# Second layer: the first product as three row-banded parts on four 32-row bands, expert 0 in 16-bit halves, all engines in program order

## The chip, the cores and the metric

The kernel runs on one core of a Trainium2 chip. Its engines are TensorE (PE, matmuls; PEld is its weight load), VectorE (DVE), ScalarE (ACT), GpSimd (POOL) and SyncE (SP, which issues DMAs). The time is device microseconds of one launch. The median of three runs before the change is 997.73 us (992.65 to 998.36).

## The reference

An mLSTM attention gives x (3072 x 320). A first mixture layer (soft, 8 experts of 4 slots) and a second one follow; the change lies in the second.

```python
def _moe_ref(x, phi, w1, w2):                 # first layer
    logits = x @ phi                          # 3072 x 32
    ...
    slot_out[e] = np.maximum(slot_input[e] @ w1[e], 0.0) @ w2[e]
    ...
    return c @ slot_out                       # c: softmax over the 32 slots

def _moe2_ref(x, w_gate, w1, w2):             # second layer, x = c @ slot_out
    P = np.exp(x @ w_gate - max)
    for _ in range(8):                        # Sinkhorn
        P /= P.sum(1, keepdims=True) + 1e-09
        P /= P.sum(0, keepdims=True) + 1e-09
        P *= N / E
    for e in range(E):                        # 8 experts, w1[e] 320 x 1024, w2[e] 1024 x 320
        h = np.maximum(x @ w1[e], 0.0)
        out += P[:, e:e + 1] * (h @ w2[e])
    return out
```

## The kernel before

The attention and the first layer's logits run up to about 199 us of the span, a tail list (TAIL) up to 207, the first layer's experts up to 237. The rest is the second layer: 48 blocks, n = 0 to 47, of 512 tokens each, six blocks an expert (e, tb = divmod(n, 6)).

The input of the second layer has rank 32: x = c @ slot_out. So x @ w1[e] is computed as c @ S with S = slot_out @ w1[e] (32 x 1024), made by s1_p (col4: four column strips of PE at once, the weights' last 64 rows on 64-row tiles) and s1_c. To keep precision c and S are each split into a rounded half and a rest. cst stacks the rounded c, a copy of it (c_m, on POOL) and the rest of c on 96 partitions; sst stacks the halves of S in the matching order. One 96-row matmul then gives all three parts: z (128 of the 1024 features x 512 tokens). c_p transposes c for a block, c_a and c_d write its halves.

A block runs g1 for eight feature groups kc (one z matmul of 96 rows; ACT writes hh = relu(z) rounded, DVE writes hl, the rest) and g2 for four token tiles tt (24 y matmuls of 320 columns: hh by wh, hh by wl and hl by wh for each kc; then DVE accumulates y into acc with the gate's factor). g1 of block n + 1 is issued in pairs after each g2 of block n. For experts 1 to 7, hh, hl, wh and wl are 16 bit, scaled by powers of two from the absolute maxima of the weights (amax, scales, prep_w2); for expert 0 they are float32r. Gates (gate_p, gate_a, gate_t, gate_d) fill Pm during block 0, and the eight Sinkhorn rounds run in blocks 2 to 5, as sinkhorn_a (row sums, then cl, the column sums, on DVE) and sinkhorn_b (psk, a small PE matmul of cl, then four DVE operations).

What sets the order: PE runs in program order all the time (man). ACT, DVE and POOL run in program order from expert 6 of the first layer to block 1 of the second (man4); after that a scheduler orders them. A PE instruction that waits holds back all that follow.

Of the kernel before, what the change touches and what calls it, by code (L numbers as in the profile page):

```python
# [21 lines left out]
def mlstm_moe_kernel(  # L22
# [37 lines left out]
    CK = 3 * NS  # L60
# [11 lines left out]
    NRB = 5  # L72
# [822 lines left out]
    cst = sm_p.tile([CK, N], F32R, name="cst")  # L895
# [20 lines left out]
    def c_p(gq, pool, tag):  # L916
        pt = pool.tile([P, 512], F32, tag=tag, name="ptc")
        for j in range(TPB):
            nc.tensor.transpose(pt[0:NS, j * P:(j + 1) * P], ct_all[:, gq, j, :], ident)
        tmp["ct", gq] = pt  # L920

    def c_a(gq):
        nc.scalar.copy(out=cst[0:32, gq * TB:(gq + 1) * TB], in_=tmp["ct", gq][0:32, :])

    def c_d(gq):
        cs = slice(gq * TB, (gq + 1) * TB)
        nc.vector.tensor_tensor(
            out=cst[64:96, cs], in0=tmp.pop(("ct", gq))[0:32, :], in1=cst[0:32, cs], op=ALU.subtract,
        )
# [90 lines left out]
    for gq in range(gl):  # L1020
        c_m(gq, gq + 1)
# [72 lines left out]
    wh = {0: wp.tile([P, KF, DM], F32R, name="wh0")}  # L1094
    wl = {0: wp.tile([P, KF, DM], F32R, name="wl0")}

    def prep_w20(k0, k1):
        for kk in range(k0, k1):
            ks = slice(2 * kk, 2 * kk + 2)
            r = w20[0].rearrange("p (k d) -> p k d", d=DM)[:, ks, :]  # L1100
            nc.scalar.copy(out=wh[0][:, ks, :], in_=r)
            nc.vector.tensor_tensor(out=wl[0][:, ks, :], in0=r, in1=wh[0][:, ks, :], op=ALU.subtract)


    scl2 = {}

    def load_w2(e):
        for kk in range(4):
# [5 lines left out]
    def amax(e, kk):  # L1114

        if kk == 0:
            tmp["mx4"] = g_p.tile([P, 2, 4], F32, tag="mx4", name="mx4", bufs=2)
        for a, src in enumerate((m2w[e][:, kk * 640:kk * 640 + 640], raw[:, 2 * kk:2 * kk + 2, :].rearrange("p a d -> p (a d)"))):
            nc.vector.tensor_reduce(  # L1119
                out=tmp["mx4"][:, a, kk:kk + 1], in_=src, axis=AX.X, op=ALU.max, apply_absolute_value=True,  # L1120
            )

    def norm_so():

        nr = g_p.tile([P, 1], F32, name="nr")
        nc.vector.tensor_reduce(out=nr, in_=soa, axis=AX.X, op=ALU.add, apply_absolute_value=True)
        tmp["nso"] = g_p.tile([P, 1], F32, name="nso")
        nc.gpsimd.partition_all_reduce(tmp["nso"], nr, P, bass_isa.ReduceOp.max)

    def scales(e):  # L1130
        mx, mr, iv, sc = (g_p.tile([P, 2], F32, tag=n, name=n, bufs=2) for n in ("mx2", "mr2", "iv2", "sc2"))
        ds = g_p.tile([P, 1], F32, tag="ds2", name="ds2", bufs=2)
        nc.vector.tensor_reduce(out=mx, in_=tmp.pop("mx4"), axis=AX.X, op=ALU.max)  # L1133
        nc.gpsimd.partition_all_reduce(mr, mx, P, bass_isa.ReduceOp.max)  # L1134
        nc.vector.tensor_scalar(
            out=mr[:, 0:1], in0=mr[:, 0:1], scalar1=tmp["nso"], scalar2=4.0, op0=ALU.mult, op1=ALU.mult,
        )
        nc.vector.tensor_scalar(
            out=mr.bitcast(I32), in0=mr.bitcast(I32), scalar1=0x7F800000, scalar2=None, op0=ALU.bitwise_and,
        )  # L1140
        nc.vector.tensor_scalar(
            out=iv, in0=mr, scalar1=1.0 / 16384.0, scalar2=1e-34, op0=ALU.mult, op1=ALU.max,
        )
        nc.vector.reciprocal(sc, iv)
        nc.vector.tensor_tensor(out=ds, in0=iv[:, 0:1], in1=iv[:, 1:2], op=ALU.mult)
        scl2[e] = sc, ds

    def prep_w2(e, k0=0, k1=4):
# [3 lines left out]
        sc = scl2[e][0][:, 1:2]  # L1152
        for kk in range(k0, k1):
            ks = slice(2 * kk, 2 * kk + 2)
            nc.scalar.activation(out=wh[e][:, ks, :], in_=raw[:, ks, :], func=AF.Copy, scale=sc)
            nc.vector.scalar_tensor_tensor(
                out=wl[e][:, ks, :], in0=raw[:, ks, :], scalar=sc, in1=wh[e][:, ks, :],
                op0=ALU.mult, op1=ALU.subtract,
            )

    def scale_p(e):
        nc.vector.tensor_scalar_mul(Ps[:, :, e], Pm[:, :, e], scl2[e][1])

    up(0)
    for e in range(E - 1):
        if e == E - 2:
# [87 lines left out]
    def g1(n, kc):  # L1254
        e, tb = divmod(n, NB)
        if kc == 0:
            hs[n] = tuple(hp.tile([P, KF, TB], F16 if e else F32R, tag=t, name=t) for t in ("hh", "hl"))
        hh, hl = hs[n]
        z = psz.tile([P, TB], F32, tag="z", name="z")
        nc.tensor.matmul(  # L1260
            z, Sst[e][:, kc * P:(kc + 1) * P], cst[:, tb * TB:(tb + 1) * TB], start=True, stop=True,
        )
        nc.scalar.activation(out=hh[:, kc, :], in_=z, func=AF.Relu)  # L1263
        nc.vector.scalar_tensor_tensor(  # L1264
            out=hl[:, kc, :], in0=z, scalar=0.0, in1=hh[:, kc, :], op0=ALU.max, op1=ALU.subtract
        )

    Pm = sm_p.tile([P, NT, E], F32, name="Pm")
    Ps = g_p.tile([P, NT, E], F32, name="Ps")

    y0 = {}

    def g2(n, tt, k0=0, k1=KF):
# [6 lines left out]
        for kc in range(k0, k1):  # L1280
            nc.tensor.matmul(y, hh[:, kc, ts], wh[e][:, kc, :], start=(kc == 0), stop=False)  # L1281
            nc.tensor.matmul(y, hh[:, kc, ts], wl[e][:, kc, :], start=False, stop=False)  # L1282
            nc.tensor.matmul(y, hl[:, kc, ts], wh[e][:, kc, :], start=False, stop=(kc == KF - 1))  # L1283
# [10 lines left out]
        if e == 1:  # L1294
            nc.vector.tensor_scalar_mul(a, a, Pm[:, i, 0:1])
# [6 lines left out]
    def gate_p(gg):  # L1302
# [30 lines left out]
    gm = sm_p.tile([P, 1], F32, name="gm")  # L1333
    ga = sm_p.tile([P, 1], F32, name="ga")
# [129 lines left out]
```

## Time and profile before

| | us |
|---|---|
| median of three runs | 997.73 |
| profiled execution | 996.21 |
| its span, first to last instruction | 994.4 |
| PE busy in the span | 935.0 |
| DVE busy | 656.3 |
| ACT busy | 412.7 |
| POOL busy | 132.5 |

The mean granted TensorE clock is 0.985 of full speed. Matmul records overlap, since matmuls are pipelined, so the distance from one start to the next tells the rate, and the record's length does not.

### The profile page before, as it was taken

To read this page: it belongs to the slowest core of one execution; us is meant where nothing else is said; L and a number is where in the kernel's file an instruction comes from. 1 tells how busy PE (TensorE), PEld (TensorE's weight loads), DVE (VectorE), ACT (ScalarE), POOL (GpSimd) and SP (SyncE) were. 2 spreads that over 40 slices of the span, in tenths; PEclk is the share of its full clock that TensorE was granted. 3 is DMA by queue.
4 is the path that set the end of the run, shared out by engine and by line. 5 is a ranking of instruction groups with operands and counts; after the bars stand their busy time and mean duration, and the time that the engine had idled before them with its cause. 6 is when DMAs were issued, how large, how long until landed. Compare 5 with 4: busy or idle time off the path is not lost.

```text
span 994.4 us, 18368 instructions
## 1 busy us (share of the span) xinstructions
PE 935.0 (94%) x7607; PEld 681.0 (68%) x7607; DVE 656.3 (66%) x1348; ACT 412.7 (41%) x782; POOL 132.5 (13%) x205
## 2 busy tenths in 40 slices
PE   3688888999998999999999999999999999999998
PEld 1477676735987976666666666666666666666665
DVE  6999999835799784666467565756564564545443
ACT  3668777734434222443334342334422442423221
POOL 3677576610000000000000000000000000000000
PEclk9979999999999999999999999999999999999999
DMA  5578887796013000100011010101010000000111
GB/s 93 97 153 158 173 169 181 223 330 210 1 54 106 1 1 1 53 27 28 11 44 53 1 54 1 54 1 54 12 43 1 1 1 2 1 1 28 40 47 47
DMA packets 129605, 63.52 MB, mean 64 GB/s; under 512 B 103507, under 2 KB 123315, under 8 KB 129523
## 3 DMA queue, kind: packets, MB, share of 16 engines
q1 hardware_dynamic: 129523, 62.37, 24.4%
q8 instruction: 59, 0.97, 0.4%
q14 instruction: 23, 0.19, 0.1%
HBM read 58.17 MB, written 4.18 MB: 63 GB/s over the span
## 4 chain that ended last, share of the span: by engine, by line
PE 80%; DVE 15%; issue 3%; ACT 1%; DMA 0%; POOL 0%; SPq 0%; DVEq 0%; POOLq 0%; ACTq 0%
PE y L1281 21%; PE y L1283 21%; PE y L1282 21%; PE z L1260 9%; DVE st L380 3%; DVE W L491 2%; PE pu L1035 2%; DVE st L386 1%; PE pd L1073 1%; DVE amx L346 1%; PE pu L1042 1%; DVE C L519 1%; DVE mx L1119 1%; PE po L544 1%; PE ptk L416 1%
## 5 line engine op out<-in xcount | busy, mean ns | idle before, releaser
L1281 PE MATMUL y<-wx,hh 128*128 128x320 f16 x1344 | 403.9, 301 | 0.0
L1283 PE MATMUL y<-wx,hl 128*128 128x320 f16 x1344 | 401.9, 299 | 0.0
L1282 PE MATMUL y<-wx,hh 128*128 128x320 f16 x1344 | 401.9, 299 | 0.0
L1263 ACT ACTIVATE hh<-z 128x512 f16<-128x512 f32 (+1 forms) x384 | 209.6, 594 | 440.9 <-PE z L1260 440.4
L1264 DVE SCALAR_TENSOR_TENSOR hl<-z,hh 128x512 f16<-128x512 f32 (+1 forms) x384 | 248.2, 686 | 51.1 <-ACT hh L1263 49.1
L1296 DVE SCALAR_TENSOR_TENSOR acc<-y,Ps,acc 128x320 f32<-128x320 f32 x168 | 92.4, 550 | 215.2 <-PE y L1283 214.9
L1281 PEld LDWEIGHTS <-hh 128*128 128x128 f16 x1344 | 131.5, 98 | 89.2 <-issue 43.0
L1283 PEld LDWEIGHTS <-hl 128*128 128x128 f16 x1344 | 131.5, 98 | 51.8 <-DVE hl L1264 1.0
L1282 PEld LDWEIGHTS <-hh 128*128 128x128 f16 x1344 | 132.0, 98 | 44.7
L1260 PE MATMUL z<-cst,sst 96*128 96x512 f32 x384 | 139.5, 442 | 2.4 <-DVE hl L1264 2.3
L1260 PEld LDWEIGHTS z<-cst,sst 96*128 96x128 f32 x384 | 63.3, 191 | 12.7 <-issue 2.9
L1134 POOL PARTITION_ALL_REDUCE mr<-mx x7 | 2.6, 367 | 454.1 <-DVE mx L1133 454.1
L1281 PE MATMUL y<-wh,hh 128*128 128x320 f32 x192 | 61.5, 320 | 0.0
L1283 PE MATMUL y<-wh,hl 128*128 128x320 f32 x192 | 60.8, 317 | 0.2 <-DVE hl L1264 0.2
L1282 PE MATMUL y<-wl,hh 128*128 128x320 f32 x192 | 60.6, 316 | 0.0
L421 ACT COPY T<-ptk 120x1024 f16<-120x1024 f16 x47 | 47.8, 1018 | 17.1 <-PE ptk L416 17.1
L380 DVE SCALAR_TENSOR_TENSOR st<-kq,asc,st 128x320 f16<-128x320 f32 x48 | 40.2, 838 | 2.1 <-ACT st L375 2.1
L416 PE MATMUL ptk<-ident,st 128*120 128x128 f16 x384 | 31.9, 230 | 10.1 <-DVE st L386 6.2
L416 PEld LDWEIGHTS <-st 128*120 128x120 f16 x384 | 30.5, 143 | 14.1 <-issue 5.6
L1282 PEld LDWEIGHTS y<-wl,hh 128*128 128x128 f32 x192 | 37.3, 194 | 0.9
L1281 PEld LDWEIGHTS y<-wh,hh 128*128 128x128 f32 x192 | 37.3, 195 | 0.6
L1283 PEld LDWEIGHTS y<-wh,hl 128*128 128x128 f32 x192 | 37.3, 194 | 0.4 <-DVE hl L1264 0.4
(245 smaller groups left out, 971.9 us busy)
## 6 DMA issues: line engine op xcount, KB each, us to landing
wa<-in_moe_w_dram SPq DMA_DIRECT2D x18, 512.0 KB, 4.5
raw<-in_moe_w_dram SPq DMA_DIRECT2D x28, 320.0 KB
xr<-in_o_gate_dram SPq DMA_DIRECT2D x24, 160.0 KB, 4.7
kq<-in_k_dram SPq DMA_DIRECT2D x24, 160.0 KB, 2.6
kq<-in_q_dram SPq DMA_DIRECT2D x24, 160.0 KB, 3.0
vz<-in_v_dram SPq DMA_DIRECT2D x24, 160.0 KB, 4.1
wb<-in_moe_w_dram SPq DMA_DIRECT2D x6, 640.0 KB, 10.4
out_dram<-acc SPq DMA_DIRECT2D x24, 160.0 KB, 1.8
```

Of the source, the lines that this page charges most:

```text
L380: nc.vector.scalar_tensor_tensor(out=st[:, a, :, lo, :], in0=t[:, a], scalar=sc[:, a:a + 1], in1=st[:, a, :, 0, :], op0=ALU.mult, op1=ALU. ...
L416: nc.tensor.transpose(pt[0:120, h, :], sts[i % (PD - 1)][:, a, h].rearrange("p s d -> p (s d)"), ident16)
L421: nc.scalar.copy(out=t, in_=tmp.pop(("k", a, i))[0:120])
L491: nc.vector.scalar_tensor_tensor(out=Ws[i][:, hh * 4:hh * 4 + 4, :], in0=tmp.pop(("s", i, hh)), scalar=scl[i][:, 0:1], in1=dds.pop((i, hh) ...
L1035: nc.tensor.matmul(dst[32 * j:32 * j + 32, :], lhsT[:, kt, :], v[:, 2 * kt + j // 2, (j % 2) * FQ:(j % 2 + 1) * FQ], start=(kt == 0), stop ...
L1260: nc.tensor.matmul(z, Sst[e][:, kc * P:(kc + 1) * P], cst[:, tb * TB:(tb + 1) * TB], start=True, stop=True,)
L1263: nc.scalar.activation(out=hh[:, kc, :], in_=z, func=AF.Relu)
L1264: nc.vector.scalar_tensor_tensor(out=hl[:, kc, :], in0=z, scalar=0.0, in1=hh[:, kc, :], op0=ALU.max, op1=ALU.subtract)
L1281: nc.tensor.matmul(y, hh[:, kc, ts], wh[e][:, kc, :], start=(kc == 0), stop=False)
L1282: nc.tensor.matmul(y, hh[:, kc, ts], wl[e][:, kc, :], start=False, stop=False)
L1283: nc.tensor.matmul(y, hl[:, kc, ts], wh[e][:, kc, :], start=False, stop=(kc == KF - 1))
L1296: nc.vector.scalar_tensor_tensor(out=a, in0=y, scalar=Ps[:, i, e:e + 1], in1=a, op0=ALU.mult, op1=ALU.add)
```

## The change

The first product no longer stacks its three parts on 96 rows. csh and csr hold the rounded half of c and the rest, each four times, on four bands of 32 partitions; sst holds the halves of S with the feature quarter j on band j. g1 now takes four feature groups at once: 12 matmuls of 32 rows, three for each of four z buffers, in the order part by part, band by band. A block has two such groups, issued after g2 of tiles 0 and 2. psz has four buffers and psy two, instead of three and three. c_p writes each transpose four times, by 16 strip matmuls; c_m goes. The gates take two matmuls a block of tokens, on 64 and on 32 rows.

Expert 0 uses 16-bit halves as the others do, so its maxima, scales and splits come before block 0. The work for the next expert (ahead2) is spread over three blocks, one step after each g2. ACT, DVE and POOL run in program order from expert 3 of the first layer to the end. The ring of weight buffers has four slots instead of five.

```diff
-    NRB = 5
+    NRB = 4
...
         for j in range(TPB):
-            nc.tensor.transpose(pt[0:NS, j * P:(j + 1) * P], ct_all[:, gq, j, :], ident)
+            for g in range(4):
+                nc.tensor.matmul(
+                    pt[NS * g:NS * g + NS, j * P:(j + 1) * P], ct_all[:, gq, j, :], ident,
+                    start=True, stop=True, tile_position=(0, NS * g),
+                )
...
-    psz = ctx.enter_context(tc.tile_pool(name="psz", bufs=3, space=PSUM, reuse_waits="tile"))
-    psy = ctx.enter_context(tc.tile_pool(name="psy", bufs=3, space=PSUM, reuse_waits="tile"))
+    psz = ctx.enter_context(tc.tile_pool(name="psz", bufs=4, space=PSUM, reuse_waits="tile"))
+    psy = ctx.enter_context(tc.tile_pool(name="psy", bufs=2, space=PSUM, reuse_waits="tile"))
...
-    wh = {0: wp.tile([P, KF, DM], F32R, name="wh0")}
-    wl = {0: wp.tile([P, KF, DM], F32R, name="wl0")}
+    wh = {0: wp.tile([P, KF, DM], F16, name="wh0")}
+    wl = {0: wp.tile([P, KF, DM], F16, name="wl0")}
...
-        if e == E - 2:
+        if e == 3:
 
             man4 = tc.manual_schedule(engines={mybir.EngineType.Activation, mybir.EngineType.DVE, mybir.EngineType.Pool})
...
+        for a, kk in {4: ((0, 0), (0, 1), (0, 2)), 5: ((0, 3), (1, 0), (1, 1)), 6: ((1, 2), (1, 3))}.get(e, ()):
+            amax(0, a, kk)
+    amax_all(0, 1)
+    amax_all(0, 0)
...
+    def s1_c(e):
+        (sh, sr), pj, sc = Sst[e], tmp.pop("s1"), sch[e][1]
+        nc.scalar.activation(out=sh, in_=pj, func=AF.Copy, scale=sc)
+        nc.vector.scalar_tensor_tensor(out=sr, in0=pj, scalar=sc, in1=sh, op0=ALU.mult, op1=ALU.subtract)
...
-        z = psz.tile([P, TB], F32, tag="z", name="z")
-        nc.tensor.matmul(
-            z, Sst[e][:, kc * P:(kc + 1) * P], cst[:, tb * TB:(tb + 1) * TB], start=True, stop=True,
-        )
...
+        zs = [psz.tile([P, TB], F32, tag="z", name="z") for _ in range(4)]
+        fs, cs = slice(t * P, (t + 1) * P), slice(tb * TB, (tb + 1) * TB)
+        for a, (w, c) in enumerate(((sh, csh), (sr, csh), (sh, csr))):
+            for j, z in enumerate(zs):
+                r = slice(32 * j, 32 * j + 32)
+                nc.tensor.matmul(
+                    z, w[r, fs], c[r, cs], start=(a == 0), stop=(a == 2), tile_position=(32 * j, 0),
+                )
...
+    KO = [0, 2, 4, 6, 1, 3, 5, 7]
...
+            for a, c in enumerate((csh, csr)):
+                r = NS * (2 - a)
+                nc.tensor.matmul(
+                    tmp["ga", gg], sgs[0:r, (3 - j) * NS:(3 - j) * NS + P],
+                    c[0:r, (b0 + j) * TB:(b0 + j + 1) * TB],
...
+    def ahead2(x):
+
+        for a in range(2):
+            for kk in range(4):
+                yield amax(x, a, kk)
+            amax_all(x, a)
+        yield
+        yield pow2(x, 0)
+        yield pow2(x, 1)
+        s1(x)
+        yield
+        for kk in range(4):
+            yield prep_w2(x, kk)
+        if x + 1 < E:
+            load_m2w(x + 1)
...
         for tt in range(TPB):
             g2(n, tt)
...
-            if n + 1 < NBLK:
-                g1(n + 1, 2 * tt)
-                g1(n + 1, 2 * tt + 1)
...
+            if n + 1 < NBLK and tt % 2 == 0:
+                g1(n + 1, tt // 2)
+            next(steps, None)
 
             st = (n - 1) * TPB + tt
             if 4 <= st < 20:
                 (sinkhorn_b if st % 2 else sinkhorn_a)()
```

How this moves instructions shows at two places. The first is PE in a block of expert 1 or later, between the y matmuls of two token tiles (an instruction of z loads its own weights, and those on 32 rows read csh or csr). Before:

```order
L1282 MATMUL y<-wx,hh 128x320
L1283 LDWEIGHTS hl
L1283 MATMUL y<-wx,hl 128x320
L1260 MATMUL z<-cst,sst 128x512 x2
L1281 LDWEIGHTS hh
L1281 MATMUL y<-wx,hh 128x320
L1282 LDWEIGHTS hh
```

Now:

```order
L1292 LDWEIGHTS hh
L1292 MATMUL y<-wx,hh 128x320
L1293 LDWEIGHTS hl
L1293 MATMUL y<-wx,hl 128x320
L1266 MATMUL z<-csh,sst 128x512 x8
L1266 MATMUL z<-csr,sst 128x512 x4
L1291 LDWEIGHTS hh
L1291 MATMUL y<-wx,hh 128x320
```

Two z matmuls stood there after every g2; now twelve stand there after every other one.

The second place is DVE around the second Sinkhorn sum (rw to cl) of blocks 2 to 5. Before, in the order that the scheduler found:

```order
L1264 SCALAR_TENSOR_TENSOR hl<-z,hh 128x512 x6
L1349 TENSOR_REDUCE rw<-Pm 128x24
L1350 TENSOR_SCALAR rw<-rw 128x24
L1351 RECIPROCAL rw<-rw 128x24
L1352 TENSOR_TENSOR Pm<-Pm,rw 128x192
L1353 TENSOR_REDUCE cl<-Pm 128x8
L1292 COPY acc<-y 128x320
L1264 SCALAR_TENSOR_TENSOR hl<-z,hh 128x512 x2
```

Now, in program order:

```order
L1302 COPY acc<-y 128x320
L1272 SCALAR_TENSOR_TENSOR hl<-z,hh 128x512 x4
L1103 TENSOR_REDUCE mx_4265<-raw 128x1
L1362 TENSOR_REDUCE rw<-Pm 128x24
L1363 TENSOR_SCALAR rw<-rw 128x24
L1364 RECIPROCAL rw<-rw 128x24
L1365 TENSOR_TENSOR Pm<-Pm,rw 128x192
L1366 TENSOR_REDUCE cl<-Pm 128x8
L1302 COPY acc<-y 128x320
L1103 TENSOR_REDUCE mx_4265<-raw 128x1
L1371 TENSOR_SCALAR ca<-psk 128x8
```

The sum stands behind four hl of a group and a maximum (mx) that belongs to expert 1, and the two accumulations of a group's tiles stand on both sides of it. On PE, psk follows the y matmuls of the tile after the group, with no z between them.

## Rows read from the trace of the kernel before

**Rows 1.** Busy time by engine in stretches, with instruction counts, granted clock and DMA share.

```profile
core 0: us, PE busy (x) PEld busy (x) DVE busy (x) ACT busy (x) POOL busy (x), PEclk, DMA share, GB/s
...
207.00:240.00 33.00, 31.06 (x383) 12.44 (x382) 12.22 (x28) 10.56 (x26) 1.22 (x3) 0.95 0.86 273
...
260.50:354.00 93.50, 87.86 (x565) 83.31 (x565) 79.48 (x185) 32.42 (x60) 1.49 (x4) 0.96 0.14 43
354.00:990.00 636.00, 636.00 (x4497) 437.14 (x4496) 364.93 (x632) 215.22 (x397) 1.43 (x4) 1.00 0.07 23
```

**Rows 2.** Timeline of PE in a steady stretch: start, length, line, operation, operands.

```profile
503.08 0.30 PE L1282 MATMUL y<-wx,hh 128*128 128x320 f16 x1
...
506.07 0.30 PE L1283 MATMUL y<-wx,hl 128*128 128x320 f16 x1
506.09 0.73 PE L1260 MATMUL z<-cst,sst 96*128 96x512 f32 x2
506.67 0.31 PE L1281 MATMUL y<-wx,hh 128*128 128x320 f16 x1
```

**Rows 3.** Timeline of the weight loads (PEld) in the same stretch.

```profile
506.07 0.33 PEld L1260 LDWEIGHTS z<-cst,sst 96*128 96x128 f32 x2
```

**Rows 4.** Timeline of PE around the strips that make S for expert 2.

```profile
401.51 0.30 PE L1283 MATMUL y<-wx,hl 128*128 128x320 f16 x1
401.74 1.07 PE L1035 MATMUL pu<-wa,soT 128*32 128x256 f32 x16
402.74 0.64 PE L1042 MATMUL pu<-wa,soT 64*32 64x256 f32 x8
403.31 0.73 PE L1260 MATMUL z<-cst,sst 96*128 96x512 f32 x2
403.88 0.31 PE L1281 MATMUL y<-wx,hh 128*128 128x320 f16 x1
```

**Rows 5.** The 64-row tail of the strips: shortest, median, longest, first and last start.

```profile
L1042 PE MATMUL pu<-wa,soT x8: 376/388/400, 402.7 to 403.0; 64*32 64x256 f32 x8
```

**Rows 6.** Waits of PE from 260 to 354 us: total, times, longest.

```profile
engine line waited for: us in total, times, longest us
PE psk L1357 <- DVE cl L1353: 3.2, 2, 1.7
```

**Rows 7.** Timeline of all engines in block 1, DVE and ACT after a pair of z.

```profile
262.82 0.34 DVE L1349 TENSOR_REDUCE rw<-Pm 128x24 f32<-128x192 f32 x1
...
264.07 0.63 PE L1260 MATMUL z<-cst,sst 96*128 96x512 f32 x2
264.13 0.55 DVE L1353 TENSOR_REDUCE cl<-Pm 128x8 f32<-128x192 f32 x1
...
264.56 1.09 ACT L1263 ACTIVATE hh<-z 128x512 fp32r<-128x512 f32 x2 [2.26 <-PE z L1260]
...
265.19 1.29 DVE L1264 SCALAR_TENSOR_TENSOR hl<-z,hh 128x512 fp32r<-128x512 f32 x2
...
266.40 0.81 DVE L1119 TENSOR_REDUCE mx<-wa 128x1 f32<-128x640 f32 x1
```

**Rows 8.** Busy time and clock in the 5 us after a wait of psk.

```profile
310.00:315.00 5.00, 5.00 (x25) 4.91 (x24) 3.83 (x10) 0.21 (x1) 0.00 (x0) 0.66 0.00 0
```

**Rows 9.** Timeline of PE at that wait.

```profile
308.98 0.39 PE L1357 MATMUL psk<-cl,ones 128*128 128x8 f32 x2 [1.65 <-DVE cl L1353]
309.22 0.40 PE L1281 MATMUL y<-wh,hh 128*128 128x320 f32 x1
```

**Rows 10.** Timeline of PE: the first y of block 1 and of block 6.

```profile
260.56 0.31 PE L1281 MATMUL y<-wh,hh 128*128 128x320 f32 x1
...
353.51 0.30 PE L1281 MATMUL y<-wx,hh 128*128 128x320 f16 x1
```

**Rows 11.** Timeline: the last two sums of the first layer on DVE, the first z.

```profile
233.10 0.55 DVE L1084 SCALAR_TENSOR_TENSOR soa<-pd,emask,soa 128x320 f32<-128x320 f32 x1 [2.60 <-PE pd L1073]
...
235.27 0.55 DVE L1084 SCALAR_TENSOR_TENSOR soa<-pd,emask,soa 128x320 f32<-128x320 f32 x1 [0.64 <-PE pd L1073]
...
240.24 0.70 PE L1260 MATMUL z<-cst,sst 96*128 96x512 f32 x2
```

**Rows 12.** Timeline of PE: two transposes of c in the tail.

```profile
198.38 1.05 PE L919 MATMUL ptc<-ident,ct_all 128*32 128x128 f32 x8
```

More of the change, by code (lines that the diff above doesn't have):

```diff
@@ L1112, in load_w2, with prep_a @@
             )
[L1114 to L1148, printed above, removed]
+    KP = [slice(0, 3, 2), slice(4, 7, 2), slice(1, 4, 2), slice(5, 8, 2)]
+    def prep_a(e, kk):
         if e not in wh:
@@ L1151, in prep_w2, with prep_d @@
             wh[e], wl[e] = wx[:, a, :, :], wx[:, a + 1, :, :]
[L1152 to L1159, printed above, removed]
+        nc.scalar.activation(out=wh[e][:, KP[kk], :], in_=src2[e][:, KP[kk], :], func=AF.Copy, scale=scw[e][1])
+    def prep_d(e, kk):
+        nc.vector.scalar_tensor_tensor(
+            out=wl[e][:, KP[kk], :], in0=src2[e][:, KP[kk], :], scalar=scw[e][1], in1=wh[e][:, KP[kk], :],
+            op0=ALU.mult, op1=ALU.subtract,
+        )
+    def prep_w2(e, kk):
+        prep_a(e, kk)
+        prep_d(e, kk)
     def scale_p(e):
-        nc.vector.tensor_scalar_mul(Ps[:, :, e], Pm[:, :, e], scl2[e][1])
+        nc.vector.tensor_scalar(
+            out=Ps[:, :, e], in0=Pm[:, :, e], scalar1=sch[e][0], scalar2=scw[e][0], op0=ALU.mult, op1=ALU.mult,
+        )
     up(0)
     for e in range(E - 1):
-        if e == E - 2:
+        if e == 3:
             man4 = tc.manual_schedule(engines={mybir.EngineType.Activation, mybir.EngineType.DVE, mybir.EngineType.Pool})
@@ L1183, in mlstm_moe_kernel @@
     c_p(gl, psp, "p")
+    pow2(0, 1)
+    prep_a(0, 0)
     down_d(E - 1)
+    norm_so()
     soT = sm_p.tile([P, 3, NS], F32, name="soT")
@@ L1279, in g2 @@
         y = y0[tt]
-        for kc in range(k0, k1):
-            nc.tensor.matmul(y, hh[:, kc, ts], wh[e][:, kc, :], start=(kc == 0), stop=False)
+        for k in range(k0, k1):
+            kc = KO[k]
+            nc.tensor.matmul(y, hh[:, kc, ts], wh[e][:, kc, :], start=(k == 0), stop=False)
             nc.tensor.matmul(y, hh[:, kc, ts], wl[e][:, kc, :], start=False, stop=False)
-            nc.tensor.matmul(y, hl[:, kc, ts], wh[e][:, kc, :], start=False, stop=(kc == KF - 1))
+            nc.tensor.matmul(y, hl[:, kc, ts], wh[e][:, kc, :], start=False, stop=(k == KF - 1))
         if k1 < KF:
@@ L1380, in mlstm_moe_kernel @@
+    for k in range(KF):
+        if k == 3:
+            g1(0, 1)
+        for tt in range(2):
+            g2(0, tt, k, k + 1)
+        if k == 3:
+            gate_p(0)
             gate_a(0)
-        elif kc == 1:
+        elif k == 5:
             gate_t(0)
             gate_d(0)
-        elif kc == 3:
-            gate_p(1)
-            gate_a(1)
-        elif kc == 4:
-            gate_t(1)
-            gate_d(1)
-        elif kc == 5:
-            gate_m()
-        if kc >= G1K:
-            g1(1, kc - G1K)
@@ L1394, in mlstm_moe_kernel @@
-    g2(0, TPB - 1)
-    for kc in range(KF - G1K, KF):
-        g1(1, kc)
+    gate_p(1)
+    gate_a(1)
+    g2(0, 2)
+    gate_t(1)
+    gate_d(1)
+    g1(1, 0)
+    g2(0, 3)
+    gate_m()
+    g1(1, 1)
     gate_e()
     NBLK = E * NB
+    def ahead2(x):
[12 more added lines that the diff above has]
+            load_m2w(x + 1)
@@ L1399, in mlstm_moe_kernel @@
     for n in range(1, NBLK):
         e, tb = divmod(n, NB)
-        if tb == 1 and 0 < e < E - 1:
-            load_w2(e + 1)
-            for kk in range(4):
-                amax(e + 1, kk)
-            scales(e + 1)
-            prep_w2(e + 1)
-        if tb == 4 and 0 < e < E - 1:
-            scale_p(e + 1)
+        if tb == (1 if e == 0 else 0) and e + 1 < E:
+            if e > 0:
+                load_w2(e + 1)
+            steps = ahead2(e + 1)
+        if tb == 0 and e > 0:
+            if e == 1:
+                scale_p(0)
+            scale_p(e)
@@ L1430, in mlstm_moe_kernel @@
                 (sinkhorn_b if st % 2 else sinkhorn_a)()
-                if st == 19:
-                    scale_p(1)
-        if n == 1:
-            man4.__exit__(None, None, None)
+    for x in steps:
+        pass
+    man4.__exit__(None, None, None)
     man.__exit__(None, None, None)
```

164 lines of the change are left out of this document (71 added, 93 removed).

## Prediction

> **What bounds the kernel now.** I read the stages first, then one steady stretch, then the waits of expert 0. By stage [rows 1], TensorE (PE) is busy 636.0 of 636.0 us between 354 and 990 us, at a granted clock of 1.00: experts 1 to 7 of the second layer, 42 blocks of 512 tokens. Nothing on VectorE (DVE) or ScalarE (ACT) counts there unless it grows by half; only what PE issues does. Between 260.5 and 354 us, blocks 1 to 5 of expert 0, PE is busy 87.86 of 93.50 us, so 5.6 us are waits.
>
> The steady stretch gives the price list [rows 2]. Second-product matmuls start every 0.136 us (503.08 to 506.07 holds 22 of them). The last before a pair of first-product matmuls starts at 506.07 and has streamed by 506.21; the next y starts at 506.67. So a pair costs 0.46 us between the streams, 0.48 counted by the 3.74 us period less 24 x 0.136. A block has 96 y matmuls and four pairs: 13.04 + 1.92 = 14.96 us. The pair's weight load is free, because it starts at 506.07 [rows 3], together with the last y.
>
> **The main term: the first product.** Before, 8 matmuls of 512 columns a block, 4 pairs. After, two groups of 12 on four 32-row bands. If the four bands run together, that is 3 rounds a group, 6 a block instead of 8. The trace has no bands of 32 rows with 128 columns. The nearest rows are the column strips of the first product's input and its 64-row tail [rows 4, 5]: 16 matmul records in four rounds take 1.00 us until the next shape starts, 8 in two rounds take 0.57. Two equations give a round of 0.215 us and 0.14 us for each change of shape. The 0.14 is a drain (y starts at 401.51, has streamed by 401.65, the strips start at 401.74: 0.09), the first weights (32 columns) and the issue. So four tiles do run at once, in the tail even on two different row bands [rows 5]: eight records start within 0.3 us.
>
> What a band group costs, by these: entry drain 0.09; first weights, now 128 columns, 0.11 (the pair after the strips takes 0.57 from 403.31 to 403.88 [rows 4], against 0.46 where its load was hidden); 0.02 issue; three rounds 0.645; exit drain 0.09; 0.03 for the first y weights. Sum 0.99 us, against 0.96 for the two pairs that it replaces. The two rounds saved in a block (0.43 us) are spent on four shape changes, each with a drain and with a weight load in the open. 84 groups belong to experts 1 to 7: 84 x 0.03 = **+2.4 us**. Bounds: with no drain and no issue a group is 0.107 + 0.645 + 0.03 = 0.78; one matmul after another it is 12 x 0.215 + 0.32 = 2.9. I take 0.99, since the strip rows are the same engine changing shape.
>
> A rule stands against one step of this. The pair's weights loaded under a y matmul on the same rows [rows 3], so I let rounds two and three hide their loads. The Trainium skill, "TensorE: Matmul & The Clock Gate", section "Part 3: Packing small matmuls", says that a load overlaps matmuls in flight only where its row group differs. By it each round would pay its load, 0.107 + 0.215, and a group 1.20 us; the rows speak against it here.
>
> **The order of work in blocks 1 to 5.** This is the second term, and the order rows show it. Each of eight Sinkhorn rounds has a column sum on DVE (cl), which PE's small psk matmul waits for, in PE's program order. Before, a scheduler set DVE's order and put most sums early; two waits of psk remained, 3.2 us together [rows 6]; the rest of the 5.6 us is a wait for z's buffers. After, DVE's order is the program's: accumulate, four hl, a maximum or a weight split, then the five Sinkhorn operations. From the end of a band group: ACT starts 0.27 us later (z at 264.07, streamed by 264.29, ACT at 264.56), hl starts 0.63 after ACT, four hl take 4 x 0.645 = 2.58 (a pair 1.29), a maximum 0.81, the sum from rw to the end of cl 1.86 (262.82 to 264.68) [rows 7]. That is 6.15 us. PE has only 24 x 0.136 = 3.26 us of work before psk, so it waits 2.9. By block: block 2 (maxima) 2 x 2.9; block 3: 2.1 (no step), then 1.1 (four small operations for a scale, some 0.7, an estimate from the four that take 1.31 between 262.82 and 264.13; but 1.8 us of strips lie ahead of psk); block 4 (weight splits, taken like a maximum) 2 x 2.9; block 5 2 x 2.1. Sum 19 us where 5.6 were.
>
> After psk's wait of 1.65 us [rows 9] the granted clock was 0.66 over the 5 us from 310 [rows 8], a mean of its two levels, 2.4 and 1.2 GHz: 1.7 us lost. The wait for z's buffers was followed by a like stretch, psk's other wait by none. Of the new waits seven are of 2 us or more; I take 9 us, between 0 and 14 (8 x 1.7).
>
> Expert 0's second product goes from float32r, 0.146 us a matmul (260.56 to 264.07 holds 24 [rows 7, 10]), to 16 bit at 0.136. Blocks 1 to 5 after: 5 x (13.04 + 2 x 0.99) = 75.1, the strips for expert 1 1.8 (403.88 - 401.51 less the usual 0.60), waits 19, psk itself 8 x 0.24 = 1.9 (308.98 to 309.22 [rows 9]), clock 9: 106.8. Before: 353.51 - 260.56 = 93.0 [rows 10]. **+13.8 us.** Who is late next after a wait: nobody, since DVE and ACT then stand idle until the next group.
>
> **Join and block 0.** Expert 0 now needs powers of two before its first split. Eight maxima sit between the down sums on DVE, from expert 4 on. Two of them, two clears and four small operations stand between expert 6's sum, which ended at 233.65, and the last one, which started at 235.27 [rows 11]: 2 x 0.81 + 0.34 + 0.7 puts it at 236.3, and soT and the first z (240.24) follow 1.0 us later. Then the z group needs both halves of the split (0.4 + 0.5, an estimate from hh and hl, which take 0.545 and 0.645 for twice the columns), and the pipeline starts with ACT's start, hh and hl in a row (0.27 + 0.63 + 0.65). The gates are 12 matmuls on 64 and 32 rows instead of 6 on 96: 12 x 0.215 without and 12 x 0.41 with a shape change each; I take 3.7. The second half of the split is then there at 241.2, and two rounds and a drain later, at 241.8, the first z: 1.6 + 13.04 + three groups 2.97 + gates 3.7 + their transposes 0.8 = 263.9 for block 1, against 260.56: **+3.5 us** (2 to 6). One weight buffer fewer (NRB 4) I cost at nothing: the queues have 14% free between 207 and 240 us [rows 1]; if that cover fails, 4.6 us (14% of 33) is the most that a fuller queue can take.
>
> **The tail of the first layer.** Each of six transposes becomes 16 strip matmuls. Two old ones took 1.05 us [rows 12], 0.53 each; a new one 4 x 0.215 + 0.14 = 1.0. Six times 0.5 is 3; half to all of it is in front of something that waits. **+2.0 us** (0 to 3). The copies by GpSimd vanish, off the path: nothing.
>
> **Sum.** 2.0 + 3.5 + 13.8 + 2.4 = 21.7 on the profiled execution's 996.2 us: **1018 us**. The median of the runs is 997.7, 1.5 above the profiled one. What a measurement here can tell from no change is about 1%.
>
> **Rivals.**
> - Not slower: PE doesn't drain between y and the bands and issues without a gap, so a group costs 0.78. Then 96 x 0.21 = 20 us come back: 998. It decides from 0.77 downward. For it: the 96-row pair enters and leaves without a drain [rows 2]. Against it: the gaps of 0.09 around every strip group [rows 4]. Chance 0.12.
> - Loads show in every round, group 1.20: 96 x 0.21 = +20, 1038. For it: no row has two loads of 128 columns in two bands. Against it: [rows 3]. Chance 0.08; this is the time that the rule above gives. A figure of the same section, 3.07 times for four bands of 512 columns, would give a group of about 1.2 as well.
> - Loads of the four bands go one after another: 12 x 0.107 + 0.215 + 0.21 = 1.71, +69 us: 1087. Strip loads, each of 32 columns, don't queue so [rows 5]. Chance 0.10.
> - The change doesn't do what it says, and the bands run in turn: 2.9 a group, +183 us: about 1200. Chance 0.04.
> - The Sinkhorn sums come early enough: -28 us (19 + 9), 990. For it: only two of eight psk waits showed before [rows 6]. Against it: its order, by which 0.9 + 2.58 + 1.86 us of work stand against PE's 3.26. Chance 0.06.
>
> **How the numbers follow.** The forecast has 0.60, and its own range is 1005 to 1026 (clock 0 to 14, tail and join by their bounds). With the first two rivals that is 0.80: 997 to 1040. Faster by over 1% (below 986): half of the last rival and corners of the first, 0.06. Within 1%: the rest of these and the low corner of the forecast, 0.17. Slower: 0.77.
>
> **What would show it.** Steady block 15.0 us with z in two bursts of about 0.65 us; starts of four z matmuls a few ns apart; a gap of 0.09 us on both sides. psk in blocks 2 to 5 waiting for cl eight times, 17 to 21 us in all, and a granted clock below 1.00 after some. First y of block 1 near 266 us. Wrong if a steady block is under 14.7 or over 15.5 us, or if psk waits under 8 us in all.

## The result and the profile after

The change makes the kernel slower: 1011.1 us in the median of four runs (1005.8 to 1011.7) against 996.7 before, ratio 1.014 with an interval of 1.010 to 1.018. In a second comparison the same kernel (again, below) took 1009.9 against 995.9, ratio 1.0153 (1.0129 to 1.0177). So the change costs some 14 us. 1018 was forecast, with a range of 997 to 1040. The profiled execution after took 1005.8 us, its span 1004.1; it was the shortest of its runs.

Where the time went, stage by stage, from timelines of the two kernels (the first column after is this profile; "again" is the second profiled execution of the changed kernel). The bounds of a stage are the start of the last-but-one sum of the attention (sacc), of the copies siT and soT on DVE (the transposed inputs and outputs of the first layer's slots), and of the first y of blocks 1, 6 and 47.

| stage, us | before | after | again | forecast of the change |
|---|---|---|---|---|
| start to sacc | 198.5 | 194.5 | 196.8 | none |
| sacc to siT (tail) | 8.7 | 10.1 | 10.1 | +2.0 |
| siT to soT (experts, join) | 29.6 | 29.7 | 29.8 | +1.0 |
| soT to block 1 (block 0) | 23.8 | 29.1 | 29.2 | +2.5 |
| blocks 1 to 5 | 93.0 | 96.8 | 96.6 | +13.8 |
| blocks 6 to 46 | 624.2 | 627.2 | 627.2 | +2.4 (to the end) |

The first row is not the change's: in the eleven profiles of the changed kernel and its edits (below), which share this stage, sacc starts anywhere from 194.5 to 199.8 us, and the 198.5 before lies among them. An operation on DVE that runs 48 times in it (st from kq) took 838 ns each before, 784 and 781 ns in the two profiles after. Without that row the change costs 13.7 us by either profile (9.7 + 4.0 and 12.0 + 1.7, from spans of 994.4, 1004.1 and 1006.4), about what the medians say.

The four rows of the timeline of DVE and PE that bound the early stages after (answering [rows 10, 11]):

```profile
194.50 0.55 DVE L699 SCALAR_TENSOR_TENSOR sacc<-sacc,sc,pq 128x321 f32<-128x321 f32 x1
...
204.58 0.26 DVE L995 TENSOR_TENSOR siT<-ptf,rs 128x96 f32<-128x96 f32 x1
...
234.29 0.26 DVE L1201 COPY soT<-pt_so 128x96 f32<-128x96 f32 x1 [0.45 <-PE pt_so L949]
...
263.40 0.31 PE L1291 MATMUL y<-wh,hh 128*128 128x320 f16 x1
```

**The steady group.** The timeline of PE after, where [rows 2] stood before, and of the weight loads, where [rows 3] stood:

```profile
524.71 0.30 PE L1293 MATMUL y<-wx,hl 128*128 128x320 f16 x1
524.94 0.74 PE L1266 MATMUL z<-csh,sst 32*128 32x512 f32 x8
525.51 0.40 PE L1266 MATMUL z<-csr,sst 32*128 32x512 f32 x4
525.84 0.31 PE L1291 MATMUL y<-wx,hh 128*128 128x320 f16 x1
```

```profile
524.58 0.10 PEld L1293 LDWEIGHTS <-hl 128*128 128x128 f16 x1
524.94 0.30 PEld L1266 LDWEIGHTS z<-csh,sst 32*128 32x128 f32 x8 [0.26 <-issue]
525.28 0.20 PEld L1266 LDWEIGHTS z<-csr,sst 32*128 32x128 f32 x4
```

From the end of a y (524.71 + 0.136) to the next y at 525.84 a group takes 0.99 us, the forecast's number. Its parts: 0.09 until the first loads, twelve matmuls in three rounds, and at the end a y whose own load starts in the open. The loads of the second round, in a narrower window, start at 525.05, while the first round streams on the same rows:

```profile
525.05 0.19 PEld L1266 LDWEIGHTS z<-csh,sst 32*128 32x128 f32 x4
```

So rounds two and three hide their loads. By the rule that was weighed in the prediction (the Trainium skill, "TensorE: Matmul & The Clock Gate", section "Part 3: Packing small matmuls") they would not, and this trace contradicts it. A steady block takes 15.05 us, 14.96 before.

**The waits.** The waits of PE after from 200 to 380 us (answering [rows 6]), and DVE and PE at one of the eight:

```profile
PE psk L1370 <- DVE cl L1366: 15.0, 8, 2.5
```

```profile
283.58 2.48 DVE L1272 SCALAR_TENSOR_TENSOR hl<-z,hh 128x512 f16<-128x512 f32 x4 [1.03 <-ACT hh L1271]
285.98 0.81 DVE L1103 TENSOR_REDUCE mx<-raw 128x1 f32<-128x640 f32 x1
286.71 0.34 DVE L1362 TENSOR_REDUCE rw<-Pm 128x24 f32<-128x192 f32 x1
...
288.03 0.49 DVE L1366 TENSOR_REDUCE cl<-Pm 128x8 f32<-128x192 f32 x1
```

```profile
286.00 0.30 PE L1293 MATMUL y<-wh,hl 128*128 128x320 f16 x1
288.67 0.36 PE L1370 MATMUL psk<-cl,ones 128*128 128x8 f32 x2 [2.37 <-DVE cl L1366]
288.88 0.30 PE L1291 MATMUL y<-wh,hh 128*128 128x320 f16 x1
```

DVE does not pause between 283.58 and the sum: it is late by its order, four hl and a maximum ahead of the sum, and PE has run out of y at 286.00. What followed the waits is in a table by stretch (columns as in [rows 1]; the 5 us behind three of the eight waits, then blocks 1 to 5, then the steady part):

```profile
288.70:293.70 5.00, 5.00 (x43) 3.34 (x44) 2.25 (x7) 0.47 (x1) 0.00 (x0) 1.00 0.00 0
299.00:304.00 5.00, 5.00 (x43) 3.33 (x44) 2.23 (x7) 0.49 (x1) 0.38 (x1) 1.00 0.02 5
...
329.00:334.00 5.00, 5.00 (x26) 3.17 (x26) 1.83 (x6) 0.00 (x0) 0.00 (x0) 0.66 0.00 0
...
263.40:360.19 96.79, 81.82 (x645) 53.55 (x641) 65.28 (x154) 26.38 (x50) 0.76 (x2) 0.98 0.09 28
...
365.00:980.00 615.00, 615.00 (x4967) 413.84 (x4965) 358.58 (x645) 186.78 (x354) 4.53 (x12) 1.00 0.08 25
```

Of the eight stretches behind a wait one shows the low clock of [rows 8], 0.66, the other seven 1.00. That is 1.7 us (0.34 x 5), where the forecast took 9.

### The profile page after: what moved, and what is told of

The parts are those of the page before. It is cut to its first block, busy times and chain, and to the rows that moved or that the text cites. A ratio compares the mean times of both kernels' runs of the same rounds, so it can differ in the third digit from the quotient of the medians.

```text
span 1004.1 us, 20232 instructions
## 1 busy us (share of the span) xinstructions
PE 936.5 (93%) x8549; PEld 642.4 (64%) x8549; DVE 646.0 (64%) x1363; ACT 378.8 (38%) x728; POOL 132.4 (13%) x205
## 4 chain that ended last, share of the span: by engine, by line
PE 76%; DVE 12%; ACT 2%; issue 2%; DMA 1%; SPq 0%; POOL 0%; DVEq 0%; ACTq 0%
PE y L1291 21%; PE y L1293 20%; PE y L1292 20%; PE z L1266 9%; DVE hl L1272 2%; DVE W L490 2%; DVE st L379 2%; DMA big<-in_moe_w_dram 1%; PE pu L1034 1%; DVE st L385 1%; DVE C L518 1%; DVE amx L345 1%; PE po L543 1%; ACT hh L1271 1%; PE po L551 1%
## 5 line engine op out<-in xcount | busy, mean ns | idle before, releaser
L1271 ACT ACTIVATE hh<-z 128x512 f16<-128x512 f32 x384 | 198.3, 602 | 490.6 <-PE z L1266 490.6
L1272 DVE SCALAR_TENSOR_TENSOR hl<-z,hh 128x512 f16<-128x512 f32 x384 | 238.5, 683 | 93.2 <-ACT hh L1271 93.1
L1291 PEld LDWEIGHTS <-hh 128*128 128x128 f16 x1536 | 151.1, 98 | 93.4 <-issue 37.4
L1292 PEld LDWEIGHTS <-hh 128*128 128x128 f16 x1536 | 150.7, 98 | 54.6
L1266 PE MATMUL z<-csh,sst 32*128 32x512 f32 x768 | 71.0, 441 | 0.6 <-ACT sst L1217 0.6
L1291 PE MATMUL y<-wh,hh 128*128 128x320 f16 x192 | 58.9, 307 | 0.7 <-ACT hh L1271 0.7
L1293 PE MATMUL y<-wh,hl 128*128 128x320 f16 x192 | 58.8, 306 | 0.3 <-DVE hl L1272 0.3
L1292 PE MATMUL y<-wl,hh 128*128 128x320 f16 x192 | 58.8, 306 | 0.0
L420 ACT COPY T<-ptk 120x1024 f16<-120x1024 f16 x47 | 47.8, 1017 | 14.9 <-PE ptk L415 14.8
L1266 PEld LDWEIGHTS z<-csh,sst 32*128 32x128 f32 x768 | 29.1, 183 | 26.2 <-issue 24.3
L1266 PE MATMUL z<-csr,sst 32*128 32x512 f32 x384 | 38.7, 392 | 0.0
L415 PEld LDWEIGHTS <-st 128*120 128x120 f16 x384 | 29.7, 140 | 13.4 <-issue 5.5
L543 PE MATMUL po<-vz,W 128*64 128x41 f32 x768 | 32.2, 234 | 5.6 <-DVE y L569 2.6
L490 DVE SCALAR_TENSOR_TENSOR W<-pss,aiv,dd 128x512 f32<-128x512 f32 x48 | 35.5, 740 | 1.1 <-PE pss L484 1.0
```

What stands on the lines that cost most here:

```text
L415: nc.tensor.transpose(pt[0:120, h, :], sts[i % (PD - 1)][:, a, h].rearrange("p s d -> p (s d)"), ident16)
L420: nc.scalar.copy(out=t, in_=tmp.pop(("k", a, i))[0:120])
L490: nc.vector.scalar_tensor_tensor(out=Ws[i][:, hh * 4:hh * 4 + 4, :], in0=tmp.pop(("s", i, hh)), scalar=scl[i][:, 0:1], in1=dds.pop((i, hh) ...
L543: nc.tensor.matmul(po[TH * a:TH * a + TH, gg, j * D1:(j + 1) * D1], Ws[i][:, h, TH * a:TH * a + TH], own_v(vz[i % NV], h, 1).rearrange("p ...
L1266: nc.tensor.matmul(z, w[r, fs], c[r, cs], start=(a == 0), stop=(a == 2), tile_position=(32 * j, 0),)
L1272: nc.vector.scalar_tensor_tensor(out=hl[:, kc, :], in0=z, scalar=0.0, in1=hh[:, kc, :], op0=ALU.max, op1=ALU.subtract)
```

## The experiments

All are edits of the changed kernel. Times are medians, ratios are to the kernel before on the same chip, with 95% intervals.

| run | us | ratio |
|---|---|---|
| again | 1009.9 | 1.0153 (1.0129 to 1.0177) |
| sums_early | 990.1 | 0.9953 (0.9936 to 0.9971) |
| two_parts | 987.6 | 0.9932 (0.9910 to 0.9954) |
| extra_shape | 1034.2 | 1.0398 (1.0378 to 1.0418) |
| extra_same | 1014.0 | 1.0191 (1.0168 to 1.0214) |
| band_major | 1011.5 | 1.0171 (1.0150 to 1.0192) |
| rows96 | 987.9 | 0.9931 (0.9913 to 0.9949) |
| gates128 | 987.7 | 0.9932 (0.9910 to 0.9955) |
| rows96_late | 991.9 | 0.9972 (0.9957 to 0.9987) |
| rows96_join | 984.4 | 0.9902 (0.9881 to 0.9923) |

### again: the changed kernel once more

No edit. 

> The changed kernel once more, for a second profile and interval. In the profiled execution (1005.8 us) the clock cost only some 3 us in blocks 1 to 5 and the attention stage was 4 us shorter than before; the other executions of it took about 1011 us at a lower mean clock. If the psk waits cost clock, this profile shows a time near 1011 with more stretches below full clock behind psk in blocks 2 to 5, the stage 5 to 10 us longer. If the difference is the attention stage's own spread, blocks 1 to 5 take the same 96.8 us and the attention stage is longer.

Blocks 1 to 5 took 96.6 us with 14.9 us of waits in eight, as in the first profile. The attention was 2.3 us longer than there: the difference between the two profiles lies in the attention, not in the clock behind psk. One stretch of eight shows the low clock here too, but another one: it follows the first wait (PE's starts 2.66 us apart), and the longest (2.80) is followed by 1.00. The waits, and the 5 us behind these two:

```profile
PE psk L1370 <- DVE cl L1366: 14.9, 8, 2.5
```

```profile
291.20:296.20 5.00, 5.00 (x26) 3.15 (x26) 1.72 (x6) 0.00 (x0) 0.00 (x0) 0.69 0.00 0
333.00:338.00 5.00, 5.00 (x42) 3.35 (x43) 2.33 (x7) 0.46 (x1) 0.00 (x0) 1.00 0.00 0
```

### sums_early: DVE's sums ahead of hl

```diff
             g2(n, tt)
+            st = (n - 1) * TPB + tt
+            if 4 <= st < 20 and st % 2 == 0:
+                sinkhorn_a()
             if n + 1 < NBLK and tt % 2 == 0:
                 g1(n + 1, tt // 2)
...
-            st = (n - 1) * TPB + tt
-            if 4 <= st < 20:
-                (sinkhorn_b if st % 2 else sinkhorn_a)()
+            if 4 <= st < 20 and st % 2:
+                sinkhorn_b()
```

> The changed kernel with the five DVE operations of each Sinkhorn sum ahead of the next group's hl in program order, and nothing else moved. If the order of DVE makes psk wait (theory), the eight waits of 15 us in all go to under 3 us, with them the slow stretches behind them, and the kernel gains 13 to 20 us on the changed one: 991 to 998 us, the same as before the change within 1%. Rival: DVE is full in blocks 2 to 5, and the wait moves to hl or to z's buffers; then it gains less than 6 us.

20 us back, with the same instructions. DVE after the edit, and blocks 1 to 5 in the table by stretch:

```profile
289.53 0.34 DVE L1362 TENSOR_REDUCE rw<-Pm 128x24 f32<-128x192 f32 x1
...
290.85 0.50 DVE L1366 TENSOR_REDUCE cl<-Pm 128x8 f32<-128x192 f32 x1
291.26 2.47 DVE L1272 SCALAR_TENSOR_TENSOR hl<-z,hh 128x512 f16<-128x512 f32 x4
```

```profile
270.45:348.75 78.30, 78.30 (x644) 53.02 (x641) 63.86 (x153) 26.39 (x50) 0.76 (x2) 1.00 0.11 35
```

The sum stands ahead of hl, PE is busy 78.30 of 78.30 us, and no psk waits. So the order of DVE made the waits, and waits and clock together were 96.8 - 78.3 = 18.5 us. hl can stand back here: its z is needed a block later.

### two_parts: one round fewer in every group

```diff
-        for a, (w, c) in enumerate(((sh, csh), (sr, csh), (sh, csr))):
+        for a, (w, c) in enumerate(((sh, csh), (sr, csh))):
```

(with stop at a == 1.) 

> The changed kernel without the third part of the first product (rounded half of S by the rest of c): 8 band matmuls a group instead of 12, so the result lacks that part. Theory: a group is 0.35 us of shape changes, first weights and issue, and 0.22 us a round; one round less saves 96 x 0.22 = 21 us, to about 990. If the cost went by matmul (issue or loads in turn), 4 of 12 of about 1.0 us would go, 32 us. If drains and loads alone made it, under 10 us.

The steady block fell from 15.05 to 14.59 us, 0.23 for each of its two groups. A group now takes 0.76 us from the end of a y (520.24 + 0.136) to the next, where it took 0.99:

```profile
520.24 0.30 PE L1293 MATMUL y<-wx,hl 128*128 128x320 f16 x1
520.47 0.74 PE L1266 MATMUL z<-csh,sst 32*128 32x512 f32 x8
521.14 0.31 PE L1291 MATMUL y<-wx,hh 128*128 128x320 f16 x1
```

Four matmuls of 512 columns a round on four bands thus take what one took in [rows 2] (0.24, half a pair): the bands run at once, and "in turn", "loads in turn" (0.43 a round for the loads alone) and "loads in every round" (0.32) fall.

### extra_shape and extra_same: the price of a change of shape

Both put a matmul of 32 columns between two y streams, behind tiles 1 and 3, 94 in all; one is on 32 rows, the other on 128.

```diff
+            elif n + 1 < NBLK:
+                xp = psp.tile([P, TB], F32, tag="p", name="xp")
+                nc.tensor.matmul(
+                    xp[:, 0:32], Sst[e][0][0:32, 0:P], csh[0:32, 0:32], start=True, stop=True, tile_position=(0, 0),
+                )
```

> The changed kernel with one more matmul of 32 rows and 32 columns behind the y matmuls of tiles 1 and 3 in every block but the last (94 in all), where no group stands; its output is not used. Theory: two shape changes, one load of 128 columns in the open and a few ns of matmul: 0.09 + 0.11 + 0.02 + 0.09 + 0.03, about 0.33 us each, +31 us, to about 1042. If the change of shape drains nothing, 0.05 to 0.14 us each: +5 to +13 us.

> The changed kernel with one more matmul at the same 94 places as extra_shape, 32 columns wide too, but on all 128 rows, so that no shape changes; its output is not used. There an extra matmul cost 0.30 us between the y streams. Theory: the shape changes and the load in the open make that price; without them the load hides under the last y matmul and an extra costs 0.03 to 0.08 us, +3 to +8 us on the changed kernel (1010). Rival: any float32r matmul between 16-bit ones costs about the same, +20 us or more.

On 32 rows it cost 24 us, on 128 rows 4, by the medians against those of again. The intervals of extra_same and again overlap; the steady block tells them apart, 15.13 us against 15.05. PE in the first, its load, and PE in the second:

```profile
546.16 0.30 PE L1293 MATMUL y<-wx,hl 128*128 128x320 f16 x1
546.39 0.28 PE L1435 MATMUL xp<-csh,sst 32*128 32x32 f32 x1
546.60 0.31 PE L1291 MATMUL y<-wx,hh 128*128 128x320 f16 x1
```

```profile
546.38 0.18 PEld L1435 LDWEIGHTS xp<-csh,sst 32*128 32x128 f32 x1 [0.26 <-issue]
```

```profile
543.87 0.30 PE L1293 MATMUL y<-wx,hl 128*128 128x320 f16 x1
543.90 0.29 PE L1435 MATMUL xp<-csh,sst 128*128 128x32 f32 x1
544.04 0.31 PE L1291 MATMUL y<-wx,hh 128*128 128x320 f16 x1
```

On 128 rows the load starts at 543.87, with the last y and under it, and the gap is 0.03 us. On 32 rows it is 0.30 us between the y streams: 0.09 until the load starts, the load in the open (0.11 by [rows 4]), and about 0.1 more until the next y, which would be the drain on the way back. The length of a steady block says about the same: 15.68 us with two, 15.05 without. The whole kernel lost 24 us and not the 31 expected, since blocks 1 to 5 took no longer (95.7 us): there psk waited 13.2 us instead of 15.0, and no wait was followed by the low clock. That closes the account of the first product: six rounds of 0.23 are 1.38 us a block, two visits of 0.30 make it 1.98, and the block has 15.05 - 13.04 = 2.01. Before it was 1.92. What two rounds fewer give, 0.54, the two visits take (0.6).

### band_major: the twelve matmuls band by band

```diff
-        for a, (w, c) in enumerate(((sh, csh), (sr, csh), (sh, csr))):
-            for j, z in enumerate(zs):
+        for j, z in enumerate(zs):
+            for a, (w, c) in enumerate(((sh, csh), (sr, csh), (sh, csr))):
```

> The changed kernel with the two loops over parts and bands exchanged: all three parts of a band before the next band, the same 12 matmuls. Theory: matmuls start in program order, and the second part of a band waits for its first, so the bands no longer overlap in full; a group goes from 1.0 toward 2.9 us, at the most +180 us; with the third part of a band beside the first of the next, ten rounds, about 2.5 us and +145 us. Rival: order does not matter, since the engine finds what can run; no change.

I expected the bands to run in turn; that was wrong. Almost nothing changed (a steady block 15.09 us against 15.05). In the program csh, csh and csr of band 0 stand ahead of the first csh of band 1; in the timeline all csh start ahead of any csr:

```profile
522.04 0.30 PE L1293 MATMUL y<-wx,hl 128*128 128x320 f16 x1
522.26 0.76 PE L1266 MATMUL z<-csh,sst 32*128 32x512 f32 x8
522.83 0.42 PE L1266 MATMUL z<-csr,sst 32*128 32x512 f32 x4
523.19 0.31 PE L1291 MATMUL y<-wx,hh 128*128 128x320 f16 x1
```

The exchanged order did reach the engine: the first matmuls of the four bands start 10 ns apart here (522.265 to 522.295) and 3 ns apart in the changed kernel (524.941 to 524.951), as fits two more matmuls between them.

### rows96: the 96-row z in the new order

The first product, the gates and the buffers as before, but program order, expert 0 in 16 bit, and the early sums.

```diff
-    csh = sm_p.tile([P, N], F32R, name="csh")
-    csr = sm_p.tile([P, N], F32R, name="csr")
+    cst = sm_p.tile([3 * NS, N], F32R, name="cst")
...
+        z = psz.tile([P, TB], F32, tag="z", name="z")
+        nc.tensor.matmul(
+            z, Sst[e][:, kc * P:(kc + 1) * P], cst[:, tb * TB:(tb + 1) * TB], start=True, stop=True,
+        )
```

> Program order for all engines, 16-bit halves for expert 0 and the early Sinkhorn sums, but the first product on 96 rows as before the change (three copies of c instead of four, a pair of z after every g2, three z and three y buffers, gates as before). Theory: a steady block is 14.96 us instead of 15.05 (-4 us), block 0 loses the shape changes of gates and groups (-4 to -6 us): 980 to 986 us, about 1.3% faster than before the change. Rival: the narrow writes of S (twelve small operations an expert in program order) hold DVE and ACT, and blocks 2, 8, 14 and so on lose 1 us or more each.

A steady block is 14.96 us again, blocks 6 to 46 take 623.3 us against 627.2: the bands lose 3.9 us there. The total missed the expectation (980 to 986) by some 2 us. In block 0 PE stood idle (below), and the granted clock was 0.50 from 246 to 252 us; how much is due to each was not separated:

```profile
243.04 0.70 PE L1267 MATMUL z<-cst,sst 96*128 96x512 f32 x2 [1.18 <-DVE sst L1221]
244.06 0.47 PE L1267 MATMUL z<-cst,sst 96*128 96x512 f32 x1 [0.31 <-DVE sst L1221]
246.54 0.45 PE L1290 MATMUL y<-wh,hh 128*128 128x320 f16 x1 [2.01 <-ACT hh L1270]
248.33 0.45 PE L1292 MATMUL y<-wh,hl 128*128 128x320 f16 x1 [1.08 <-DVE hl L1271]
```

### rows96_late: the same with the sums late

The edit of sums_early undone in rows96. 

> rows96 with the Sinkhorn sums back behind hl and the step, as in the change. Theory: the wait of psk comes from the work that program order puts ahead of the sum. With a pair of z after every tile only two hl stand there: 0.27 + 0.63 + 1.29 + 0.8 + 1.86 = 4.9 us against 3.26 + 0.46 us of PE work, a wait of 1.1 us where a step stands and 0.4 where none does; eight waits of 6 to 8 us in all, and rows96_late is 5 to 9 us slower than rows96 (988). Rival: the band groups make the waits; then there is no difference.

It costs 4 us (the two intervals don't overlap; blocks 1 to 5 take 82.0 us for 78.3), where the same order cost 20 us with the bands: psk waits 3.2 us in four waits instead of 15.0 in eight. That is less than the 5 to 9 us, and half of the waiting, that were expected.

```profile
PE psk L1366 <- DVE cl L1362: 3.2, 4, 1.5
```

With pairs only two hl (1.29 us) stand ahead of the sum, with groups four (2.48). Most of the loss in blocks 1 to 5 so belongs to the late sums and the groups of four together.

### gates128: the gate matmuls on 128 rows, with the early sums

```diff
-                    tmp["ga", gg], sgs[0:r, (3 - j) * NS:(3 - j) * NS + P],
-                    c[0:r, (b0 + j) * TB:(b0 + j + 1) * TB],
-                    start=(j == 0 and a == 0), stop=(j == n - 1 and a == 1), tile_position=(0, 0),
+                    tmp["ga", gg], sg_[:, (3 - j) * NS:(3 - j) * NS + P], c[:, (b0 + j) * TB:(b0 + j + 1) * TB],
+                    start=(j == 0 and a == 0), stop=(j == n - 1 and a == 1),
```

> sums_early with the gates' 12 matmuls on 128 rows, the weights of the unused rows zero, so that no gate matmul changes the shape. They stood 0.43 us apart on 64 and 32 rows in turn. Theory: 0.215 to 0.24 each, block 0 gets 2 to 3 us shorter; the whole kernel 987 us against 990, within what the intervals can tell. Rival: the gates wait for something else there, and block 0 keeps its length.

PE's timeline, first of the changed kernel, then of this one:

```profile
243.97 0.49 PE L1319 MATMUL pgl<-csh,sgs 64*128 64x512 f32 x1
244.40 0.49 PE L1319 MATMUL pgl<-csr,sgs 32*128 32x512 f32 x1
244.81 0.49 PE L1319 MATMUL pgl<-csh,sgs 64*128 64x512 f32 x1
```

```profile
246.12 0.40 PE L1321 MATMUL pgl<-csr,sgr 128*128 128x512 f32 x1
246.36 0.39 PE L1321 MATMUL pgl<-csh,sgs 128*128 128x512 f32 x1
```

0.42 us apart where the rows change between 64 and 32, 0.24 where they stay: 12 matmuls save some 2.2 us. The total's gain over sums_early is as large (2.5 us by the medians, 2.1 by the ratios, as the chips differ), but the intervals of the two overlap.

### rows96_join: rows96 with the start of block 0 interleaved by hand

```diff
-    for kc in range(3):
-        g1(0, kc)
-    prep_w2(0, 2)
-    prep_w2(0, 3)
+    s1_c(0, (1,), False)
+    g1(0, 0)
+    g1(0, 1)
+    prep_w2(0, 1)
+    s1_c(0, (2,), False)
+    g1(0, 2)
```

(False: the copy of the third part goes to GpSimd; the other two splits and preparations follow inside the loop over kc.) 

> rows96 with the start of block 0 interleaved by hand: a quarter of S, two z, the next quarter, and the weight splits behind them, the third copies on GpSimd. In rows96 PE stood still for some 6 us between the strips of S and the first y matmuls. Theory: 3 to 5 us of that go, 983 to 985 us. Rival: the splits of expert 0's weights are what block 0 waits for, and they only move: within 1 us of rows96.

984.4 us, 1% under the kernel before, the lowest median of all, and within what was expected. Its first y stands 1.58 us behind the first z, 3.50 in rows96. By the ratios the gain over rows96 is 2.9 us, and the intervals of the two overlap a little.

## Why the forecast was right, step by step

**The main term** was right in size and in mechanism: 0.99 us a group by the trace, four bands at once, loads hidden in rounds two and three, a drain and a load in the open on each visit. One step of it was given no reason: the round of 0.215 us was read from strips of 256 columns and used for bands of 512. It held (0.23 by two_parts), as half a pair, 0.24, would have suggested; but the prediction does not argue it so, and that part is luck. All four rivals about the group fall: no drain (0.09 is there, extra_shape), loads in every round and loads in turn (525.05, two_parts), bands in turn. Blocks 6 to 46 lost 3.0 us against before and 3.9 against rows96, for a forecast of 2.4.

**Blocks 1 to 5** were right in mechanism (DVE's program order, shown by sums_early) and wrong in size: +3.8 us for +13.8. The step that went wrong in size is "I take 9 us, between 0 and 14" for the clock: in either profile one wait of eight was followed by the low clock, 1.7 us. The rate came from three waits of the kernel before, two of them followed by the low clock, which is too few. The length of a wait does not decide: in the first profile the low clock followed the longest (PE's starts 2.80 us apart) and none of three of 2.65 to 2.68 us, in the second one of 2.66 and not the one of 2.80. What decides stays open. The waits were also smaller, 15.0 us by the trace where 17 to 21 was to be the sign: the starts around them stand 1.00 to 2.80 us apart, 17.4 us for eight, less 0.136 each 16.3 us for a forecast of 19, in part since four hl take 2.48 and a maximum gives way after 0.73, not 2.58 and 0.81, and since PE starts its 24 y some 0.12 us behind the end of the last band matmul (the way back, which the group's price has and this sum left out). The rest of the sum held: 75.1 + 1.8 + 1.9 = 78.8 forecast without waits and clock, 78.3 in sums_early.

**Join and block 0** were +5.4 for +3.5 (the sum there, 263.9 - 260.56, is 3.3). The join was nothing (0.1 for 1.0): the last sum of the first layer came 3.3 us after the one before it, 2.2 before the change, as the maxima between them would have it; but that one came 1.0 us sooner behind siT. Why it did was not tried. Block 0 was +5.3: the gates took the upper of the two bounds (0.42 us each, 12 x 0.41, where I took 3.7 us in all), and the clock granted was 0.72 from 246 to 252 us, which had no term:

```profile
246.00:252.00 6.00, 6.00 (x27) 3.53 (x27) 0.56 (x2) 0.59 (x1) 0.00 (x0) 0.72 0.00 0
```

The y there start 0.27 us apart from 247.46 on, just behind the gates, at 1.2 GHz. That the gates cause it is only a guess. For it: gates128 shows 1.00 from 240 to 258 us. Against it: sums_early had 0.50 from 240 to 246 us, ahead of them, and rows96, with the gates on 96 rows as before, 0.50 from 246 to 252, ahead of its gates too. The cause stays open, and these are single profiles.

**The tail** was +1.4 for +2.0.

The rival "sums early enough" did not happen, and sums_early shows that it was priced right (990 forecast, 990.1). In all the forecast's 21.7 us were 8 too many: 10.0 in blocks 1 to 5 (7.3 for the clock, 2.7 for the waits) and 1.5 in the tail and the join, against 2.8 too few in block 0 and 0.6 in the steady part. That these partly cancel is luck. The weight buffers (four instead of five) and the z and y buffers were not tried by themselves; the stage of the first layer's experts, which reads the ring, took as long as before (29.7 us for 29.6).

## What to carry to other kernels

Row tiling pays by the rounds that it saves, less what it costs to change the shape and back: here 0.23 us a round against 0.30 us a visit, so two rounds saved in two visits give nothing. By these prices products of one shape should stand together, so that fewer visits are paid; that was not tried. Where engines run in program order, a small result that another engine waits for belongs ahead of bulk work that is needed a block later; five small instructions moved past four large ones were worth 20 us here, about what the tiling could have saved with free changes of shape (two rounds of 0.23 us in each of 48 blocks, 22 us).

## What was not expected of the hardware

The engine does not hold a matmul for a free band behind one for a busy band: in band_major all four bands started within 0.03 us, though two more matmuls of each band stood ahead of the next band's first. So it is a wait for another engine, as psk's for cl (286.00 to 288.67 us), that holds back what follows on PE, and not a wait for a band. And a change between 64 and 32 rows at the same first row already costs 0.18 us a matmul (0.42 against 0.24).
